# A second layer by Strassen's seven products, with the row normalisation moved ahead of the first layer

## The chip, the cores and the metric

The kernel runs on one core of one Trainium2 chip. The metric is the device time of one execution in microseconds, the lower the better. Before the change three runs took 326.28, 327.08 and 329.61 us, a median of 327.08 us.

## The reference, cut to what matters

Two stages, one after the other: sliding-window attention with a linear bias, then a layer normalisation and two matrix products with a ReLU between them, added to the attention's output.

```python
# q, k, v: (8 batches, 8 heads, 576 rows, 64); window = 128
scores = q @ k.T / 8 + bias          # bias falls with distance, one slope per head
scores = where((rel >= 0) & (rel < window), scores, -1e9)
x = softmax(scores) @ v              # heads side by side: (8, 576, 512)
...
mu, var = mean(x), mean((x - mu) ** 2)
xn = (x - mu) / sqrt(var + 1e-06) * g_ln
ch = maximum(xn @ w_ch1, 0) @ w_ch2  # w_ch1: 512 x 2048, w_ch2: 2048 x 512
out = x + ch
```

## The kernel before

**Blocks.** The 4608 rows are 36 blocks of 128 rows, numbered n = 0 to 35 in the list `order`: nine for each of four pairs of batches. The ninth block of a pair (8, 17, 26, 35; `T` in the code) holds the last 64 rows of both batches.

**Attention of a block.** `turn` transposes the queries and keys of two blocks on TensorE (64 small transposes), into two PSUM banks that DVE and ACT copy out, two copies each. `scores` makes the products of queries and keys (32 matmuls into the banks `ps_sc`), with an exponential on ACT for each half. `masks` multiplies the exponentials by the decay of the bias on DVE, one instruction for each half. `values` multiplies by v on TensorE in two halves of four heads, each into a PSUM bank of its own. On DVE a reciprocal and a scaling then write the half of the fp16 tile x, and the scaling also sums it up (`accum_out`). `centre` makes the mean of these sums, subtracts it (xc), and starts a DMA transpose of xc into the tile xT of the block's group.

**MLP of a group.** Blocks are taken in groups: `GROUPS` has four of 2 blocks, four of 3 and four of 4. `mlp1(g)` makes the 16 slices of the hidden layer: four matmuls each, as wide as the group has rows, then a ReLU on ACT (on DVE for those named in `on_dve`) into `ht`. Since the mean alone is taken off ahead of it, `mlp2(g)` makes 16 matmuls of 512 columns for each block, and `finish` multiplies by the row's `rstd` and adds x in one DVE instruction and issues the two stores on SP's queue. The `rstd` comes from `variance` (two DVE instructions for each block) and `inv_std` (nine small DVE instructions for a whole group: a shift, a subtraction and two Newton steps).

**What sets the order.** The order on TensorE, ACT and DVE is the program's own (`manual_schedule`). Attention is a list of steps, and `weave_at(units, *places)` runs a generator of the MLP unit by unit and puts the next step of that list after each unit named in places. POOL, which issues all loads, and SP, which issues stores and DMA transposes, are put in order by the framework.

**PSUM.** There are eight banks: four belong to the two `ps_sc` tiles, and the four of `ps_mm` are shared by `mlp1`, `mlp2`, `values` and `turn`. A bank is free again when its last reader has ended.

Of the kernel before, what the change touches and what calls it, by code (L numbers as in the profile page):

```python
# [10 lines left out]
FP16 = mybir.dt.float16  # L11
# [11 lines left out]
T = 8  # L23
NSLOT = 9
HALF = P // 2
GROUPS = [2] * 4 + [3] * 4 + [4] * 4

NV = 10
AHEAD = 6
# [28 lines left out]
def kernel(  # L58
# [21 lines left out]
    def pool(name, bufs, **kw):  # L80
        return ctx.enter_context(tc.tile_pool(name=name, bufs=bufs, **kw))
# [2 lines left out]
    raw_pool = pool("raw", 4)  # L84
    turned_pool = pool("turned", 3)
    probs_pool = pool("probs", 4)
    x_pool = pool("x", 14)
    xc_pool = pool("xc", 4)
    small = pool("small", 4)
    group_pool = pool("group", 3)  # L90
    hidden_pool = pool("hidden", 2)
    out_pool = pool("outp", 4)
    ps_scores = pool("ps_scores", 1, space=PSUM)
    ps_mm = pool("ps_mm", 4, space=PSUM)

# [16 lines left out]
    def decay(m, at):  # L112
# [17 lines left out]
    ones = consts.tile([P, 4 * P], FP16)  # L130
    moments = consts.tile([P, NPAIR * NSLOT, nc.vector.BN_AGGR_DIM], FP32)
    rstd = consts.tile([P, NPAIR * NSLOT], FP32)
    w1 = consts.tile([P, NKB, FFN], FP16)
    w1g = consts.tile([P, NKB, FFN], FP16)
    w2 = consts.tile([P, NFB, DM], FP16)
    vext = [
        consts.tile([P, H, D + 1], FP16, name=f"vx{i}", tag=f"vx{i}")
        for i in range(NV)
# [10 lines left out]
    def gain_w1(first, n):  # L149

        for part in range(first, first + n):
            c, kb = divmod(part, NKB)
            cols = slice(c * W1C, (c + 1) * W1C)
            nc.vector.tensor_scalar(
                out=w1g[:, kb, cols],
                in0=w1[:, kb, cols],
                scalar1=g_sb[:, kb : kb + 1],
                scalar2=None,
                op0=ALU.mult,
            )  # L160

    def load_w2(c):
        n = NFB // 4
# [54 lines left out]
            issued += 1  # L218


    xs = {}

    turned = {}

# [101 lines left out]
    def attend(p, blk, keys, mask, tag, hps):  # L326

        heads = slice(2 * hps[0], 2 * hps[-1] + 2)
        nk = len(keys)
        if hps[0] == 0:
            pr = probs_pool.tile([P, H, nk, P], FP16, tag=tag, name=tag)
            for t, o in enumerate(keys):
                weights_of.setdefault((p, blk), []).append((pr, t, o))
        else:
            pr = weights_of[p, blk][-1][0]
        banks = ps_sc[len(scored) % 2]  # L340
        scored.append((p, blk))
        ps = banks.rearrange("p j (n t q) -> p j n t q", n=len(hps), t=nk)
        qt, b = turned["q", p, blk // 2], blk % 2
        for n, hp in enumerate(hps):
            for t, o in enumerate(keys):
                kt = turned["k", p, o // 2][:, o % 2]
                for c, r, queries in seen(p, blk, o, t):
                    cols = slice(c * HALF, (c + 1) * HALF)
                    for j in range(2):
                        rows = slice(j * HALF, (j + 1) * HALF)  # L350
                        nc.tensor.matmul(  # L351
                            in_halves(ps[cols, j, n, t, :])[:, r, queries],
                            kt[rows, hp, cols],
                            in_halves(qt[rows, b, hp])[:, r, queries],
                            start=True,
                            stop=True,
                        )
        dst = pr[:, heads].rearrange("p h t q -> p h (t q)")
        nc.scalar.activation(  # L359
            out=dst.rearrange("p (n j) q -> p j n q", j=2),  # L360
            in_=ps.rearrange("p j n t q -> p j n (t q)"),
            func=AF.Exp,
            scale=inv_sqrt_d,
        )
        unmasked.setdefault((p, blk), []).append((dst, mask[:, heads, :]))
# [23 lines left out]
    def values(p, blk, hg):  # L389

        if hg == 0:
            xs[p, blk] = x_pool.tile([P, DM], FP16, tag="x", name="x")
            sums[p, blk] = small.tile([P, 2], FP32, tag="sum", name="sum")
        ps = ps_mm.tile([P, 4, D + 1], FP32, tag="mm", name="ps_pv")
        terms = weights_of[p, blk]
        for i in range(4):
            h = 4 * hg + i
            for n, (pr, t, o) in enumerate(terms):
                nc.tensor.matmul(  # L399
                    ps[:, i, :],  # L400
                    pr[:, h, t, :],
                    vext[(p * NSLOT + o) % NV][:, h, :],
                    start=(n == 0),
                    stop=(n == len(terms) - 1),
                )
        rec = small.tile([P, 4], FP32, tag="rec", name="rec")
        nc.vector.reciprocal(out=rec, in_=ps[:, :, D])  # L407
        nc.vector.scalar_tensor_tensor(  # L408
            out=xs[p, blk][:, hg * 4 * D : (hg + 1) * 4 * D].rearrange(
                "p (h d) -> p h d", h=4  # L410
            ),
            in0=ps[:, :, 0:D],
            scalar=1.0,
            in1=rec.unsqueeze(2).broadcast_to([P, 4, D]),
            op0=ALU.mult,
            op1=ALU.mult,
            accum_out=sums[p, blk][:, hg : hg + 1],
        )

    turned_x = {}  # L420

    centred = {}

    def centre(p, blk):
# [12 lines left out]
        if p == 0 and blk < FIRST:  # L437
            nc.vector.scalar_tensor_tensor(
                out=xc,
                in0=xs[p, blk],  # L440
                scalar=mean,
                in1=g_row,
                op0=ALU.subtract,
                op1=ALU.mult,
            )
        else:
            nc.vector.tensor_scalar(  # L447
                out=xc, in0=xs[p, blk], scalar1=mean, scalar2=None, op0=ALU.subtract
            )
        n = p * NSLOT + blk  # L450
        g, at = home[n]
        if at == 0:
            turned_x[g] = group_pool.tile([P, NKB, 4 * P], FP16, tag="xT", name="xT")
        if n < BY_DMA:
            centred[p, blk] = xc
        else:
            nc.sync.dma_start_transpose(
                out=turned_x[g][:, :, at * P : (at + 1) * P], in_=xc
            )

    def turn_x(g, at, p, blk, copy):

# [130 lines left out]
    def mlp1(g, on_dve=()):  # L593
# [4 lines left out]
        for fb in range(NFB):  # L598
            ps = ps_mm.tile([P, 4 * P], FP32, tag="mm", name="ps_m1")
            for kb in range(NKB):  # L600
                nc.tensor.matmul(  # L601
# [3 lines left out]
                    start=(kb == 0),  # L605
                    stop=(kb == NKB - 1),
                )
            if fb in on_dve:
# [7 lines left out]
            else:  # L616
                nc.scalar.activation(  # L617
                    out=ht[:, fb, 0:cols], in_=ps[:, 0:cols], func=AF.Relu
                )
            yield cols  # L620

    def mlp2(g, parts=((0, NFB),)):

# [2 lines left out]
        for first, end in parts:  # L626
            for at, (p, blk) in enumerate(members[g]):
# [12 lines left out]
                if end == NFB:  # L640
                    finish(p, blk, sums[at])
                    yield DM

    def finish(p, blk, ps):
        n = p * NSLOT + blk
        o = out_pool.tile([P, DM], FP32, tag="o", name="o")
        nc.vector.scalar_tensor_tensor(  # L647
            out=o,
            in0=ps,
# [2 lines left out]
            op0=ALU.mult,  # L652
            op1=ALU.add,
        )
        for b, t0, w, p0 in spans(p, blk):
            dst, src = out[b, t0 : t0 + w, :], o[p0 : p0 + w, :]
            if blk == T:
# [6 lines left out]
    def weave_at(units, *places, group=None):  # L664


        size = len(members[group]) if group else 0
        first = sum(GROUPS[:group])
        for u, _ in enumerate(units):
            if u % 2 and u // 2 < size:  # L670
                variance(first + u // 2)
                if u // 2 == size - 1:
                    inv_std(first, size)
            advance_to(done + places.count(u))


    nc.vector.memset(ones, 1.0)
# [1 line left out]
        nc.vector.memset(vx[:, :, D : D + 1], 1.0)  # L679
    nc.vector.memset(magic, 0x5F3759DF)  # L680
    nc.vector.memset(one_line, 1.0)
    decay(m_full, 0)
    decay(m_tail, 4)
    load_until(place[3])
    engine = mybir.EngineType
    with tc.manual_schedule(engines={engine.PE}):
        with tc.manual_schedule(engines={engine.Activation, engine.DVE}):
# [6 lines left out]
            weave_at(mlp2(2), 0, 2, 4, 6, 7)  # L694


            weave_at(mlp1(3, (9, 10, 11)), 8, 12)
            weave_at(mlp2(3), 1, 2, 5, 6)
# [35 lines left out]
```

## Time and profile before

| what | value |
|---|---|
| runs, median (three) | 327.08 us (326.28 to 329.61) |
| span of the profiled execution | 326.4 us |
| group 9 (blocks 26 to 29) with its share of attention, 230.69 to 263.94 us | 33.25 us |
| last `mlp1`, 294.10 to 307.91 us | 13.81 us |
| last `mlp2`, 307.91 to 321.74 us | 13.83 us |
| relu of 128x512 on ACT (L617) | 597 ns |
| relu of 128x256 on ACT (L617) | 384 ns |
| copies of a turned block (L267, L268) | DVE 416 and 722 ns, ACT 591 and 761 ns |
| copy of a turned `T` block (L273) | DVE 726 ns, ACT 742 ns |
| small instructions of `inv_std` on DVE | 162 to 170 ns |
| store: issue to landing | 3.0 us |
| DMA transpose of xc: issue to landing | 4.5 us |

The profile shows one execution. PE is TensorE, PEld its weight loads, DVE the vector engine, ACT the scalar engine, POOL the engine that issues the loads, SP the queue for the stores. A line such as L631 is a line of the kernel. "Busy" adds up the durations of instructions; those of matmuls overlap, so the pace of a run of matmuls is read from its length in the chain of waits divided by its number. PEclk is the share of the full clock that TensorE was granted.

### The profile page before, as it was taken

The page shows a single profiled execution, that of the slowest core. Times are in us where ns is not written, and L with a number is a line of the kernel's source. Part 1 is how long each engine was busy: PE and PEld are TensorE (multiplying, and loading weights), DVE is VectorE, ACT ScalarE, POOL GpSimd, SP SyncE. Part 2 cuts the span into 40 slices and gives each one's busy share as a digit, 9 for nine tenths or more (in the row PEclk, how much of TensorE's full clock was granted, in tenths as well). Part 3 has the DMA queues.
Part 4 walks back from the last instruction along what each step waited for, and adds up shares of the span by engine and source line. Part 5 has one row for each costly group of instructions (what it writes and reads, how often), then busy time and mean ns, then how long its engine had stood idle before and what let it go on. Part 6 is the DMA issues. An engine that isn't in the chain of part 4 may idle for free.

```text
span 326.4 us, 9878 instructions
## 1 busy us (share of the span) xinstructions
PE 315.1 (97%) x4190; PEld 181.1 (55%) x4190; DVE 202.4 (62%) x633; ACT 186.3 (57%) x316; POOL 93.1 (29%) x132
## 2 busy tenths in 40 slices
PE   8889999999999999999999999999999999999994
PEld 2468655757655555556565564555455545544441
DVE  2588778776782793688577379459645864436011
ACT  6587756667757557458647547735475537205500
POOL 8823757767120540452332152120000000000000
PEclk9799999999999999999999999999999999999999
DMA  9999999999891996899299299384211430141032
GB/s 113 173 207 192 191 121 167 204 145 134 92 148 30 77 168 83 51 147 134 29 168 129 14 125 157 32 62 90 64 19 18 97 67 18 28 99 36 0 66 64
DMA packets 101726, 32.31 MB, mean 99 GB/s; under 512 B 92849, under 2 KB 97073, under 8 KB 101682
## 3 DMA queue, kind: packets, MB, share of 16 engines
q0 software_dynamic: 79872, 18.36, 68.3%
q1 hardware_dynamic: 21810, 13.32, 21.0%
q8 instruction: 33, 0.54, 0.8%
q14 instruction: 11, 0.09, 0.1%
HBM read 36.90 MB, written 9.44 MB: 142 GB/s over the span
## 4 chain that ended last, share of the span: by engine, by line
PE 85%; DVE 5%; DMA 4%; POOL 3%; issue 1%; POOLq 0%
PE ps_m L631 39%; PE ps_m L601 35%; DMA w<-in_moe_w_ch_dram 4%; PE ps_pv L399 4%; PE ps_sc L351 3%; PE ps_tr L248 3%; DVE x L408 2%; DVE rec L407 1%; POOL q L184 1%; POOL vx L194 1%; POOL k L184 1%; POOL w L145 1%; DVE o L647 0%; PE ps_tx L467 0%; PE ps_sc L248 0%
## 5 line engine op out<-in xcount | busy, mean ns | idle before, releaser
L631 PE MATMUL ps_m<-w,ht 128*128 128x512 f16 x576 | 132.5, 380 | 0.0
L617 ACT ACTIVATE ht<-ps_m 128x384 f16<-128x384 f32 (+2 forms) x183 | 89.8, 491 | 55.3 <-PE ps_m L601 52.7
L601 PE MATMUL ps_m<-xT,w1g 128*128 128x512 f16 (+2 forms) x640 | 114.3, 337 | 0.2 <-DVE probs L370 0.2
L601 PEld LDWEIGHTS <-w1g 128*128 128x128 f16 x640 | 61.8, 98 | 49.1 <-issue 0.8
L631 PEld LDWEIGHTS <-ht 128*128 128x128 f16 x576 | 53.4, 98 | 59.8
L359 ACT ACTIVATE probs<-ps_sc 128x1024 f16<-128x1024 f32 x56 | 54.2, 1021 | 46.2 <-PE ps_sc L351 46.1
L194 POOL DMA_DIRECT2D vx<-in_v_dram x40 | 33.9, 855 | 86.4 <-PE ps_pv L399 54.4
L407 DVE RECIPROCAL rec<-ps_pv 128x4 f32<-128x4 f32 x72 | 12.9, 180 | 63.5 <-PE ps_pv L399 63.3
L647 DVE SCALAR_TENSOR_TENSOR o<-ps_m,rstd,x 128x512 f32<-128x512 f32 x36 | 26.7, 745 | 29.9 <-PE ps_m L631 29.9
L370 DVE TENSOR_TENSOR probs<-probs,m 128x1024 f16<-128x1024 f16 x56 | 36.4, 682 | 1.6 <-ACT probs L359 1.3
L184 POOL DMA_DIRECT2D q<-in_q_dram x40 | 27.1, 684 | 28.2 <-PE ps_tr L248 21.3
L408 DVE SCALAR_TENSOR_TENSOR x<-ps_pv,rec 128x256 f16<-128x256 f32 x72 | 30.5, 424 | 2.5
L184 POOL DMA_DIRECT2D k<-in_k_dram x40 | 26.9, 685 | 5.1 <-DMA w<-in_moe_w_ch_dram 3.1
L472 DVE BATCH_NORM_STATS2 st<-x 128x6 f32<-128x512 f16 x36 | 24.1, 668 | 0.0
L399 PEld LDWEIGHTS <-probs 128*128 128x128 f16 x448 | 18.7, 97 | 6.6 <-DVE probs L370 0.3
L351 PE MATMUL ps_sc<-q,k 64*64 64x128 f16 (+1 forms) x1088 | 20.1, 210 | 0.7 <-ACT probs L359 0.4
L399 PE MATMUL ps_pv<-vx,probs 128*128 128x65 f16 x448 | 20.1, 193 | 0.0
L359 ACT ACTIVATE own<-ps_sc 128x1024 f16<-128x1024 f32 x12 | 11.9, 1030 | 11.8 <-PE ps_sc L351 11.8
L351 PEld LDWEIGHTS <-k 64*64 64x64 f16 x1088 | 14.8, 109 | 5.9 <-issue 3.5
L601 PE MATMUL ps_m<-xT,w 128*128 128x256 f16 x128 | 15.1, 273 | 0.4 <-ACT ht L617 0.2
L601 PEld LDWEIGHTS <-w 128*128 128x128 f16 x128 | 12.0, 98 | 2.1 <-DMA w<-in_moe_w_ch_dram 0.8
L447 DVE TENSOR_SCALAR xc<-x,mean 128x512 f16<-128x512 f16 x32 | 12.0, 375 | 1.1
(57 smaller groups left out, 190.3 us busy)
## 6 DMA issues: line engine op xcount, KB each, us to landing
out_dram<-o SPq DMA_DIRECT2D x72, 128.0 KB, 3.0
q<-in_q_dram POOLq DMA_DIRECT2D x32, 128.0 KB, 5.4
k<-in_k_dram POOLq DMA_DIRECT2D x32, 128.0 KB, 5.8
vx<-in_v_dram POOLq DMA_DIRECT2D x32, 128.0 KB, 5.9
w<-in_moe_w_ch_dram POOLq DMA_DIRECT2D x8, 512.0 KB, 12.4
q<-in_q_dram POOLq DMA_DIRECT2D x8, 64.0 KB, 5.4
k<-in_k_dram POOLq DMA_DIRECT2D x8, 64.0 KB, 4.7
vx<-in_v_dram POOLq DMA_DIRECT2D x8, 64.0 KB, 4.5
```

The lines of the kernel that those rows point to most:

```text
L184: nc.gpsimd.dma_start(out=t[b * n // 2 : (b + 1) * n // 2], in_=src[2 * p + b, :, i * P : i * P + n, :].rearrange("h (c r) d -> c h r d", ...
L194: nc.gpsimd.dma_start(out=vx[p0 : p0 + n, :, 0:D], in_=v[b, :, t0 : t0 + n, :].rearrange("h p d -> p h d"),)
L351: nc.tensor.matmul(in_halves(ps[cols, j, n, t, :])[:, r, queries], kt[rows, hp, cols], in_halves(qt[rows, b, hp])[:, r, queries], start=Tr ...
L359: nc.scalar.activation(out=dst.rearrange("p (n j) q -> p j n q", j=2), in_=ps.rearrange("p j n t q -> p j n (t q)"), func=AF.Exp, scale=in ...
L370: nc.vector.tensor_tensor(out=dst, in0=dst, in1=mask, op=ALU.mult)
L399: nc.tensor.matmul(ps[:, i, :], pr[:, h, t, :], vext[(p * NSLOT + o) % NV][:, h, :], start=(n == 0), stop=(n == len(terms) - 1),)
L408: nc.vector.scalar_tensor_tensor(out=xs[p, blk][:, hg * 4 * D : (hg + 1) * 4 * D].rearrange("p (h d) -> p h d", h=4), in0=ps[:, :, 0:D], s ...
L472: nc.vector.bn_stats(out=st, in_=xs[order[n]])
L601: nc.tensor.matmul(ps[:, 0:cols], w[:, kb, fb * P : (fb + 1) * P], xT[:, kb, 0:cols], start=(kb == 0), stop=(kb == NKB - 1),)
L617: nc.scalar.activation(out=ht[:, fb, 0:cols], in_=ps[:, 0:cols], func=AF.Relu)
L631: nc.tensor.matmul(sums[at], ht[:, fb, at * P : (at + 1) * P], w2[:, fb, :], start=(fb == 0), stop=(fb == NFB - 1),)
L647: nc.vector.scalar_tensor_tensor(out=o, in0=ps, scalar=rstd[:, n : n + 1], in1=xs[p, blk], op0=ALU.mult, op1=ALU.add,)
```

## The change

The 28 blocks from block 8 on are computed in another way; the first eight stay as they were.

- Groups become six of 2 blocks and six of 4. Groups 4 to 11 (`FAST` = 4) use the new second layer.
- `stats(n)` and `normal(n)` take the place of `centre` and `inv_std` for these blocks: mean and variance by `variance` on DVE, two small POOL instructions (an addition and a power) for `rstd`, and one DVE instruction that subtracts and scales, followed by the DMA transpose. Each block's attention is now three steps (V: values, scores, turn; M: masks and stats; N: normal) where it was two. The sum of `accum_out` and the mean fall away.
- `combine_w2` makes four combinations of the quarters of w2, once, on DVE: eight instructions of 128x1024, woven into `mlp1(4)`. Three go into memory of w1, one over a quarter of w2 itself.
- `combine_hidden` makes four sums of quarters of `ht` for each group, in two halves: eight DVE instructions, four after unit 10 of `mlp1`, four in `fast_mlp2`. For these groups `mlp1` makes the slices of the two halves of the hidden layer in turns.
- `fast_mlp2` makes seven products of half-size matrices in place of eight. Each has 8 matmuls of 256 columns for each pair of rows' blocks. Three of the products add to the bank of an earlier one (`x`, `z`), after DVE has read it. Eight additions on DVE take the banks over into the output tiles; the four blocks' stores go out in two lots.
- The places in `weave_at` are new, and no ReLU of groups 4 to 11 runs on DVE.

```diff
-GROUPS = [2] * 4 + [3] * 4 + [4] * 4
+GROUPS = [2] * 6 + [4] * 6
+FAST = 4
...
+            for dst, a, b in (
+                (t1, quarter(0, 1), quarter(0, 0)),
+                (t2, quarter(1, 1), t1),
+                (t3, quarter(1, 1), quarter(0, 1)),
+                (t4, quarter(1, 0), t2),
+            ):
+                nc.vector.tensor_tensor(
+                    out=dst[:, f], in0=a[:, f], in1=b[:, f], op=ALU.subtract
+                )
+                yield
...
+    def normal(n):
+        xc = xc_pool.tile([P, DM], FP16, tag="xc", name="xc")
+        nc.vector.tensor_scalar(
+            out=xc,
+            in0=xs[order[n]],
+            scalar1=moments[:, n, 0:1],
+            scalar2=rstd[:, n : n + 1],
+            op0=ALU.subtract,
+            op1=ALU.mult,
+        )
+        nc.sync.dma_start_transpose(out=group_tile(n), in_=xc)
+
+    def stats(n):
+        variance(n)
+        here = rstd[:, n : n + 1]
+        nc.gpsimd.tensor_tensor(
+            out=here, in0=moments[:, n, 1:2], in1=powers[:, 0:1], op=ALU.add
+        )
+        nc.gpsimd.tensor_tensor(out=here, in0=here, in1=powers[:, 1:2], op=ALU.pow)
...
-        step = first_half + second_half
+        step = first_half + second_half[:1]
...
-        steps.append([m for t in (n + 1, n + 2) if t < count for m in masks_of(t)])
+        steps.append(
+            [m for t in (n + 1, n + 2) if t < count for m in masks_of(t)] + [(stats, n)]
+        )
+        steps.append([(normal, n)])
...
+            if g >= FAST and u == 10:
+                for i in range(4):
+                    combine_hidden(g, 0, i)
...
+        dst, a, b, op = (
+            (s1, a21, a22, ALU.add),
+            (s2, s1, a11, ALU.subtract),
+            (s4, a12, s2, ALU.subtract),
+            (s3, a11, a21, ALU.subtract),
+        )[i]
+        nc.vector.tensor_tensor(out=dst[:, f], in0=a[:, f], in1=b[:, f], op=op)
...
+        def product(name, lhs, rhs, first):
+            if first:
+                banks[name] = ps_mm.tile([P, 2, QD], FP32, tag="mm", name="ps_f")
+            for pair in range(pairs):
+                for fb in range(QF):
+                    nc.tensor.matmul(
+                        banks[name][:, pair, :],
+                        lhs[:, fb, pair * P : (pair + 1) * P],
+                        rhs[:, fb, :],
...
+                yield DM
...
+        combine_hidden(g, 1, 0)
+        combine_hidden(g, 1, 1)
+        yield from product("x", a[0][0], quarter(0, 0), True)
+        add("x", 0, 0, True)
+        combine_hidden(g, 1, 2)
+        yield from product("y", a[0][1], quarter(1, 0), True)
+        add("y", 0, 0, False)
+        combine_hidden(g, 1, 3)
+        yield from product("z", s[0], t1, True)
+        add("z", 1, 1, True)
+        yield from product("x", s[1], t2, False)
+        add("x", 0, 1, True)
+        yield from product("z", s[3], quarter(1, 1), False)
+        add("z", 0, 1, False)
+        send(0)
+        yield from product("x", s[2], t3, False)
+        add("x", 1, 0, True)
+        add("x", 1, 1, False)
+        yield from product("w", a[1][1], t4, True)
+        add("w", 1, 0, False)
+        send(1)
...
-            for g in range(4, len(GROUPS)):
-                in_first = g in (6, 8, 9, 10)
-                weave_at(mlp1(g, (9,) * in_first), *(8, 10) * in_first, group=g)
-                weave_at(mlp2(g), *((1, 2, 5, 6, 9, 10) if g < 10 else (1, 2, 5, 6)))
+            weave_at(mlp1(3, (9, 10, 11)), 8, 12, 13)
+            weave_at(mlp2(3), 0, 1, 2, 4, 5, 6)
+            for g in range(4, 6):
+                weave_at(mlp1(g), 1, 4, 6, 8, 11, 13, also=range(0, 16, 2) if g == 4 else ())
+                weave_at(fast_mlp2(g), 1, 3, 5)
+            for g in range(6, len(GROUPS)):
+                weave_at(mlp1(g), 1, 2, 5, 7, 9, 12, 14)
+                weave_at(fast_mlp2(g), 3, 6, 8, 9, 13)
```

More of the change, by code (lines that the diff above doesn't have):

```diff
@@ L135 @@
     w2 = consts.tile([P, NFB, DM], FP16)
+    QF, QD = NFB // 2, DM // 2
+    hsum = [consts.tile([P, QF, 2 * P], FP16, name=f"hs{i}", tag=f"hs{i}") for i in range(2)]
+    spare = [w1[:, i, :].rearrange("p (f d) -> p f d", d=QD) for i in range(4)]
+    hsum.append(spare[3])
     vext = [
@@ L160, in gain_w1, with quarter, combine_w2 @@
             )
+    def quarter(i, j):
+        return w2[:, i * QF : (i + 1) * QF, j * QD : (j + 1) * QD]
+    t1, t2, t4 = spare[:3]
+    t3 = quarter(0, 1)
+    def combine_w2():
+        for part in range(2):
+            f = slice(part * QF // 2, (part + 1) * QF // 2)
+            for dst, a, b in (
[8 more added lines that the diff above has]
+                yield
     def load_w2(c):
@@ L416, in values @@
             op1=ALU.mult,
-            accum_out=sums[p, blk][:, hg : hg + 1],
+            **(
+                dict(accum_out=sums[p, blk][:, hg : hg + 1])
+                if (p, blk) in sums
+                else {}
+            ),
         )
@@ L597, in mlp1 @@
         ht = hidden[g] = hidden_pool.tile([P, NFB, 4 * P], FP16, tag="ht", name="ht")
-        for fb in range(NFB):
+        turn_about = chain(*zip(range(QF), range(QF, NFB)))
+        for u, fb in enumerate(turn_about if g >= FAST else range(NFB)):
             ps = ps_mm.tile([P, 4 * P], FP32, tag="mm", name="ps_m1")
@@ new lines, in fast_mlp2, with rows, add, send @@
+    def fast_mlp2(g):
+        pairs = len(members[g]) // 2
+        n0 = sum(GROUPS[:g])
+        outs = [out_pool.tile([P, 2, DM], FP32, tag="o", name="o") for _ in range(2)]
+        def rows(i):
+            if pairs == 1:
+                return x_pairs[n0 // 2][:, i : i + 1, :], outs[0][:, i : i + 1, :]
+            return x_pairs[n0 // 2 + i], outs[i]
+        banks = {}
+        def product(name, lhs, rhs, first):
[7 more added lines that the diff above has]
+                        rhs[:, fb, :],
+                        start=(first and pair == 0 and fb == 0),
+                        stop=(fb == QF - 1),
+                        skip_group_check=True,
+                    )
+                yield DM
+        def add(name, i, j, to_x):
+            x, o = rows(i)
+            cols = slice(j * QD, (j + 1) * QD)
+            nc.vector.tensor_tensor(
+                out=o[:, :, cols],
+                in0=banks[name][:, 0:pairs, :],
+                in1=(x if to_x else o)[:, :, cols],
+                op=ALU.add,
+            )
+        def send(i):
+            _, o = rows(i)
+            for at in range(pairs):
+                store(*members[g][i * pairs + at], o[:, at, :])
+        a = [[hidden_quarter(g, i, j) for j in range(2)] for i in range(2)]
+        s = [hidden_sum(g, i) for i in range(4)]
+        combine_hidden(g, 1, 0)
[19 more added lines that the diff above has]
+        send(1)
@@ L662, in finish, with weave_at @@
                     nc.sync.dma_start(out=dst[r], in_=src[r * HALF : (r + 1) * HALF])
-    def weave_at(units, *places, group=None):
-        size = len(members[group]) if group else 0
-        first = sum(GROUPS[:group])
+    def weave_at(units, *places, also=()):
         for u, _ in enumerate(units):
[L670 to L673, printed above, removed]
             advance_to(done + places.count(u))
+            if u in also:
+                next(combined, None)
     nc.vector.memset(ones, 1.0)
```

60 lines of the change are left out of this document (39 added, 21 removed).

## The prediction

> **What bounds the kernel now.** First the page's busy times and slices, then the chain that ended last, by line.
>
> ```profile
> PE 315.1 (97%) x4190; PEld 181.1 (55%) x4190; DVE 202.4 (62%) x633; ACT 186.3 (57%) x316; POOL 93.1 (29%) x132
> PE   8889999999999999999999999999999999999994
> PEclk9799999999999999999999999999999999999999
> PE ps_m L631 39%; PE ps_m L601 35%; DMA w<-in_moe_w_ch_dram 4%; PE ps_pv L399 4%; PE ps_sc L351 3%; PE ps_tr L248 3%; DVE x L408 2%; DVE rec L407 1%; POOL q L184 1%; POOL vx L194 1%; POOL k L184 1%; POOL w L145 1%; DVE o L647 0%; PE ps_tx L467 0%; PE ps_sc L248 0%
> ```
>
> TensorE is busy throughout at full clock; the second layer (L631) is 39% of the chain. Matmul durations overlap, so the pace comes from the chain in order of time (start, length, what).
>
> ```profile
> 28.23 7.87 PE ps_m L601 x72
> ...
> 307.91 13.83 PE ps_m L631 x64
> ...
> 321.76 0.75 DVE o L647
> ```
>
> A matmul of 512 columns costs 13.83/64 = 216.1 ns and one of 256 columns 7.87/72 = 109.3 ns, each with its own weight load. Next the stages: length, busy time of PE, PEld, DVE, ACT and POOL, granted clock, DMA, GB/s. The last two rows are from the start of the run.
>
> ```profile
> 94.64:120.11 25.47, 25.38 (x353) 15.12 (x354) 16.16 (x52) 15.34 (x25) 7.08 (x10) 1.00 0.86 91
> 230.69:263.94 33.25, 33.16 (x418) 17.52 (x416) 21.15 (x65) 18.46 (x26) 0.00 (x0) 1.00 0.25 50
> ...
> 8.00:10.00 2.00, 1.40 (x34) 0.79 (x33) 0.66 (x2) 0.71 (x1) 2.00 (x3) 0.64 1.95 161
> 10.00:12.00 2.00, 2.00 (x36) 0.97 (x35) 0.63 (x2) 0.71 (x2) 1.83 (x4) 0.51 1.93 170
> ```
>
> In a four-block group (second row) TensorE has 33.16 of 33.25 us and DVE 21.15, or 64%. That third of DVE is all the room that the change has. The prices on DVE:
>
> ```profile
> L370 DVE TENSOR_TENSOR probs<-probs,m 128x1024 f16<-128x1024 f16 x56 | 36.4, 682 | 1.6 <-ACT probs L359 1.3
> L408 DVE SCALAR_TENSOR_TENSOR x<-ps_pv,rec 128x256 f16<-128x256 f32 x72 | 30.5, 424 | 2.5
> L647 DVE SCALAR_TENSOR_TENSOR o<-ps_m,rstd,x 128x512 f32<-128x512 f32 x36 | 26.7, 745 | 29.9 <-PE ps_m L631 29.9
> L472 DVE BATCH_NORM_STATS2 st<-x 128x6 f32<-128x512 f16 x36 | 24.1, 668 | 0.0
> L407 DVE RECIPROCAL rec<-ps_pv 128x4 f32<-128x4 f32 x72 | 12.9, 180 | 63.5 <-PE ps_pv L399 63.3
> L447 DVE TENSOR_SCALAR xc<-x,mean 128x512 f16<-128x512 f16 x32 | 12.0, 375 | 1.1
> L473 DVE BATCH_NORM_AGGREGATE moments<-st 128x2 f32<-128x6 f32 x36 | 6.6, 182 | 1.3
> ```
>
> Last the timeline of one turned block and of the end.
>
> ```profile
> 248.14 1.94 ACT L359 ACTIVATE probs<-ps_sc 128x1024 f16<-128x1024 f32 x2 [1.93 <-PE ps_sc L351]
> 249.96 0.59 ACT L267 COPY q<-ps_tr 128x512 f16<-128x512 f16 x1
> 250.29 1.28 DVE L370 TENSOR_TENSOR probs<-probs,m 128x1024 f16<-128x1024 f16 x2
> 250.43 0.77 ACT L268 COPY k<-ps_tr 128x512 f16<-128x512 f16 x1
> ...
> 322.54 1.11 SPq L658 DMA_DIRECT2D out_dram<-o  x2
> ```
>
> **What TensorE saves.** Before, 28 blocks x 16 matmuls x 216.1 ns = 96.8 us. After, 28 matmuls of 256 columns for each block: 784 x 109.3 ns = 85.7 us. Gain 11.1 us. Other widths keep their price per column (10.40 us for 64 of 384 columns, 162.5 ns).
>
> [...]
>
> **What DVE gains and loses.** A new sum of 1024 fp16 elements has the form of L370: 682 ns. One of 512 I take at 415, being 682 less half of the 512 columns' worth (0.52 ns each). An addition out of PSUM of 512 fp32 lies between L647's 745 and the 674 ns of the copy into g_row: 690; of 256 columns, 420. For a four-block group this gives 8 reciprocals 1.4, 8 scalings 3.4, two turned blocks' copies 2.3, 8 masks 5.5, statistics 3.4, normal 1.5, and new 8 sums 5.5 and 8 additions 5.5. That is 28.4 us of DVE against TensorE's 64 x 216.1 + 112 x 109.3 ns + 5.3 of attention = 31.4. Room remains, but 90% of an engine that takes its work in order will be late in places.
>
> Groups 4 and 5 are worse. Each has two blocks of MLP but three of attention (V12 to V14, V15 to V17). Group 4: reciprocals 1.1, scalings 2.5, copies 1.9, masks 4.1, statistics 2.6, normal 1.1, sums 3.3, additions 3.4, and the eight combinations of w2 5.5: 25.4 us. Group 5: 19.7 us. TensorE needs (64 + 56) x 109.3 ns + 4.2 = 17.3 us for each. DVE's excess is 45.1 - 34.7 = 10.4 us, and it reaches TensorE: z of group 4 needs the first sum, which stands behind all of that, and `values` need their banks back. I add 1.3 us for DVE's own waits (for POOL, for products): **loss 11.7**. Lower bound: a pair of masks took 1.28 instead of 1.36, so 6% off the total, and 2 us of it may slip into group 6: 5.7. Upper bound 16.
>
> **Banks in groups 7, 8 and 9.** Here V with a turn follows y. TensorE would do values 0.48, scores 0.47 and turn 0.69, and start z 1.64 us after y. But x and y hold two of the four banks (y's addition stands behind V's work on DVE), values and then turn have the other two, and in the order of the built kernel z's first matmul waits for ACT: it gets the bank that ACT copies out last. That is 0.48 + 0.24 for half of the scores + 0.18 + 1.94 exponentials + 0.59 + 0.77 copies + 0.1 = 4.3 us after y: 2.7 lost in groups 7 and 8, and 2.0 in 9, whose `T` block has one copy of 742 ns. **Loss 7.4.** Before, the same V stood inside one open sum, which needs no new bank, and hid this.
>
> **In order on DVE, group 6.** Ahead of V20's reciprocal stand M19, N19, four sums and an addition; z waits 0.8 us for its bank, and the turn behind V21 another 1.0. **Loss 1.8.** N waits for POOL's two small instructions. No row has these: DVE's of 128x4 take 162 ns, POOL's load issues 684 to 855. I take 0.8 us for the pair, between 0.3 and 1.7; one such wait in a group is uncovered, so the ends are 3 us less and 5 us more in all. POOL's queued loads wait meanwhile, but they run six blocks ahead.
>
> **The rest.** In `mlp2(3)` N9 stands behind POOL and ahead of V10's reciprocal, whose banks the turn needs: 1.1. ACT takes over the last ReLUs: 16 x 0.60 + 2 x 1.94 + 1.4 = 14.9 us beside 16.2 of TensorE in `mlp1` of group 8, hidden. At the end four stores are issued in place of two, 0.55 us each: 1.1; the last addition (0.69) replaces `finish` (0.75). Powers' memsets (about 0.1) lie before the first load lands. What DVE no longer does (mean 214 ns, accumulator read 83, Newton steps 165) is already left out of the counts above.
>
> **Sum.** -11.1 + 11.7 + 7.4 + 1.8 + 1.1 + 1.1 = +12.0 on a span of 326.4: 338.4. The median of the runs lies 0.7 above the span: 339.
>
> **Rivals.**
> 1. *Faster (0.22).* DVE's additions and sums end ahead of the products everywhere, so TensorE is never held: 326.4 - 11.1 + 1.1 + 0.7 = 317, up to 323 with part of the bank waits. For it: DVE sits idle 38% now, and neighbours start before the last one ends. It decides at all losses together under 7.8 us; the bank waits alone are 7.4, and groups 4 and 5 would need instructions a quarter shorter than their rows.
> 2. *No change (0.13).* DVE keeps to the lower bound in groups 4 and 5 and the other ends are low: losses 10 to 12, 324 to 329.
> 3. *Much slower (0.05).* The two rows with clock 0.64 and 0.51 show that TensorE loses half its clock for 4 us after a sparse stretch; that costs 2 us. One in each of groups 4 to 9 adds 12: 351. For it: z of group 4 waits 3.5 us by my walk. Against: the other waits are at most 2.7.
>
> [...] The trace shows the drop in the two rows, but not which gap sets it.
>
> **How the numbers follow.** The forecast has 0.60, with a range of its own from 331 to 346 by the ends above. Over all cases 320 to 346 leaves out about half of rival 1, rival 3 and the tail: 0.18. About 1% is what a measurement here can tell from no change; below 323.8 lies 0.22, up to 330.3 another 0.13, and above it 0.65.
>
> **What would show it.** DVE near 240 us in all, 42 or more of 47 us busy in groups 4 and 5, which would take 47 in place of 35; TensorE idle for DVE ahead of group 4's z (3 us and more) and for ACT's copies ahead of z in groups 7, 8 and 9; the last `fast_mlp2` 12.2 us against 13.83. I am wrong if 256-column matmuls differ from 109 ns, if z doesn't wait there, or if DVE has idle time in group 4.

## The result and the profile after

The changed kernel takes 336.44 us (median of four runs, 336.04 to 337.82), the kernel before 326.89 beside it. The ratio is 1.029, with a 95% interval from 1.0245 to 1.0335: slower. The profiled execution has a span of 334.7 us against 326.4, or 8.3 more.

The page of the changed kernel, the lines that answer to those shown of before: busy times, slices of TensorE and its clock, and the chain that ended last by line.

```profile
PE 307.1 (92%) x4526; PEld 214.8 (64%) x4526; DVE 241.9 (72%) x583; ACT 184.8 (55%) x320; POOL 115.8 (35%) x188
...
PE   8889999999897698899999979997999999999992
...
PEclk9999999999999899999999999999999999999998
...
PE ps_m L664 30%; PE ps_f L756 22%; PE ps_m L697 7%; ACT probs L389 4%; PE ps_pv L433 4%; PE ps_sc L381 3%; DVE probs L400 3%; DVE x L442 2%; PE ps_tr L277 2%; DMA k<-in_k_dram 2%; DVE st L530 2%; DVE hs L732 1%; DVE w L186 1%; ACT k L297 1%; DVE o L769 1%
```

TensorE is busy 8.0 us less, and idle 334.7 - 307.1 = 27.6 us where it was idle 11.3: 16.3 us more. DVE is on the chain now. The slices show where: 13, 14 and 16 lie in groups 4 and 5, one of them with a lower clock (8 in the row PEclk), and single slices follow later on. The stages in figures, with the columns length, then busy time of PE, PEld, DVE, ACT and POOL, granted clock, DMA share, GB/s. The rows are `mlp2(3)`, group 4, group 5 and group 7.

```profile
84.36:95.40 11.04, 9.53 (x186) 5.44 (x184) 9.04 (x22) 6.35 (x10) 5.23 (x9) 1.00 0.64 76
95.40:120.69 25.29, 20.15 (x362) 16.75 (x360) 22.73 (x54) 13.39 (x26) 11.14 (x17) 0.93 0.98 82
120.69:141.91 21.22, 18.61 (x386) 15.67 (x384) 18.03 (x49) 12.69 (x25) 11.63 (x20) 1.00 1.17 108
174.76:208.53 33.77, 31.65 (x466) 22.21 (x464) 25.61 (x56) 18.42 (x27) 11.79 (x20) 1.00 0.85 99
```

In groups 4 and 5, 7.75 us of 46.51 have no TensorE work at all. Group 7 had 2.1 idle, group 8 the same. The end, from the chain in order of time:

```profile
316.62 12.24 PE ps_f L756 x112
...
328.88 0.69 DVE o L769
```

12.24 us for 112 matmuls is 109.3 ns each, and 1.59 us less than the 13.83 of the plain layer: the product side is as priced. Behind the last addition come 334.7 - 329.57 = 5.1 us, where before had 326.4 - 322.51 = 3.9.

Now the waits, in the timeline of one value product in `mlp2(3)`:

```profile
86.30 0.18 DVE L531 BATCH_NORM_AGGREGATE moments<-st 128x2 f32<-128x6 f32 x1
...
86.56 0.19 POOL L485 TENSOR_TENSOR rstd<-moments,powers 128x1 f32<-128x1 f32 x1 [5.76 <-DVE moments L531]
...
86.83 0.55 POOL L488 TENSOR_TENSOR rstd<-rstd,powers 128x1 f32<-128x1 f32 x1
...
87.42 0.41 DVE L472 TENSOR_SCALAR xc<-x,moments,rstd 128x512 f16<-128x512 f16 x1 [0.94 <-POOL rstd L488]
87.74 0.17 DVE L441 RECIPROCAL rec<-ps_pv 128x4 f32<-128x4 f32 x1
...
88.52 0.44 PE L277 MATMUL ps_tr<-iden,q 64*64 64x64 f16 x30 [1.51 <-DVE rec L441]
```

The statistics end at 86.48, GpSimd makes rstd in two instructions, and the normalisation (L472) can't start before 87.42. DVE takes its work in order, so it stands idle for 0.94 us with the next block's reciprocal and scaling, both ready, behind the waiting instruction. The bank that they would free is the one TensorE's transposes need: TensorE waits 1.51 us. In the run with the normalisation one value product later (below) this wait is 0.19 us, and `mlp2(3)` takes 9.72 us in place of 11.04. The two other large waits, by the timeline of TensorE:

```profile
113.28 0.61 PE L756 MATMUL ps_f<-w,hs 128*128 128x256 f16 x4 [2.48 <-DVE hs L732]
...
198.74 1.47 PE L756 MATMUL ps_f<-w,hs 128*128 128x256 f16 x12 [1.55 <-ACT k L297]
```

The first is z of group 4, waiting for a hidden sum; the second is z of group 7, waiting for the bank that ACT copies out last.

### The profile page after: what moved, and what is told of

Same layout as the page of the kernel before. It is cut to its first block, busy times and chain, and to the rows that moved or that the text cites. A ratio compares the mean times of both kernels' runs of the same rounds, so it can differ in the third digit from the quotient of the medians.

```text
span 334.7 us, 10542 instructions
## 1 busy us (share of the span) xinstructions
PE 307.1 (92%) x4526; PEld 214.8 (64%) x4526; DVE 241.9 (72%) x583; ACT 184.8 (55%) x320; POOL 115.8 (35%) x188
## 4 chain that ended last, share of the span: by engine, by line
PE 69%; DVE 16%; ACT 6%; POOL 3%; issue 2%; DMA 2%; POOLq 0%; DVEq 0%
PE ps_m L664 30%; PE ps_f L756 22%; PE ps_m L697 7%; ACT probs L389 4%; PE ps_pv L433 4%; PE ps_sc L381 3%; DVE probs L400 3%; DVE x L442 2%; PE ps_tr L277 2%; DMA k<-in_k_dram 2%; DVE st L530 2%; DVE hs L732 1%; DVE w L186 1%; ACT k L297 1%; DVE o L769 1%
## 5 line engine op out<-in xcount | busy, mean ns | idle before, releaser
L664 PE MATMUL ps_m<-xT,w1g 128*128 128x512 f16 (+1 forms) x640 | 117.4, 337 | 5.0 <-ACT k L297 3.4
L680 ACT ACTIVATE ht<-ps_m 128x512 f16<-128x512 f32 (+1 forms) x187 | 90.4, 498 | 56.8 <-PE ps_m L664 50.6
L756 PE MATMUL ps_f<-w,ht 128*128 128x256 f16 x448 | 51.5, 273 | 0.5 <-DVE o L769 0.5
L756 PEld LDWEIGHTS <-ht 128*128 128x128 f16 x448 | 43.5, 98 | 7.5 <-issue 0.9
L756 PE MATMUL ps_f<-w,hs 128*128 128x256 f16 x224 | 26.7, 276 | 5.9 <-ACT k L297 3.0
L697 PE MATMUL ps_m<-w,ht 128*128 128x512 f16 x128 | 31.0, 380 | 0.0
L756 PEld LDWEIGHTS <-hs 128*128 128x128 f16 x224 | 21.9, 99 | 9.2 <-issue 3.1
L769 DVE TENSOR_TENSOR o<-ps_f,x 128x512 f32<-128x512 f32 (+1 forms) x32 | 19.7, 615 | 10.3 <-PE ps_f L756 10.3
L472 DVE TENSOR_SCALAR xc<-x,moments,rstd 128x512 f16<-128x512 f16 x28 | 11.5, 412 | 18.2 <-POOL rstd L488 18.2
L769 DVE TENSOR_TENSOR o<-ps_f,o 128x512 f32<-128x512 f32 (+1 forms) x32 | 19.4, 612 | 3.8 <-PE ps_f L756 3.7
```

Source lines behind the costliest of these rows:

```text
L664: nc.tensor.matmul(ps[:, 0:cols], w[:, kb, fb * P : (fb + 1) * P], xT[:, kb, 0:cols], start=(kb == 0), stop=(kb == NKB - 1),)
L680: nc.scalar.activation(out=ht[:, fb, 0:cols], in_=ps[:, 0:cols], func=AF.Relu)
L697: nc.tensor.matmul(sums[at], ht[:, fb, at * P : (at + 1) * P], w2[:, fb, :], start=(fb == 0), stop=(fb == NFB - 1),)
L756: nc.tensor.matmul(banks[name][:, pair, :], lhs[:, fb, pair * P : (pair + 1) * P], rhs[:, fb, :], start=(first and pair == 0 and fb == 0), ...
L769: nc.vector.tensor_tensor(out=o[:, :, cols], in0=banks[name][:, 0:pairs, :], in1=(x if to_x else o)[:, :, cols], op=ALU.add,)
```

## The experiments

Each short diff is against the changed kernel, unless another is named. All times are medians, and the kernel before lay between 326.68 and 327.08 us beside them.

**The value product one unit later** (groups 6 to 11):

```diff
-                weave_at(fast_mlp2(g), 3, 6, 8, 9, 13)
+                weave_at(fast_mlp2(g), 4, 6, 8, 9, 13)
```

> In groups 6 to 11 the step V of the second layer stands one unit later, between the two halves of product z, so that z takes its bank before values and turn take theirs. Theory of the banks: z no longer waits for ACT's last copy (3.89 us from y's end to z in group 7, 3.72 in group 8, against 1.5 of TensorE's own work); 2.3 us come back in groups 7 and 8 and about 1 in group 9, where the wait was partly for DVE: 330.5 to 332 us, and TensorE's waits for ACT's copies ahead of products go from 3.0 us to 0. Rival, DVE's order: the sums and additions behind V are late anyway, so the wait only moves to the next product: 335 to 337 us.

334.0 us, ratio 1.0225 (1.0189 to 1.0261): 2.4 us less, between the two expectations. Groups 7, 8 and 9 took 32.50, 32.45 and 32.85 us in place of 33.77, 33.57 and 32.94, which is 2.5 us, and no z waits for ACT any more. So the mechanism is right and its price about half of what was expected.

**Without the sums of w2.** This leaves out the eight subtractions of w2's quarters, so the products read other weights.

```diff
-    combined = combine_w2()
+    combined = iter(())
```

> The eight combinations of w2 are left out (the products use what lies in their places). Theory of DVE's amount: group 4 takes 25.3 us with DVE busy for 22.7; without 5.4 us of it the wait of 2.5 us ahead of z goes, and with it the clock's drop behind it (25.3 us at a mean of 0.93, so 1.8 us): group 4 near 20 us, total 330.5 to 331.5. Rival, waiting and not work: DVE's queue is held by single waits, so that less work leaves the same waits: group 4 near 24 us, total 334.5 to 335.5.

332.71 us, ratio 1.0196 (1.0139 to 1.0253), between the two expectations. Group 4 fell from 25.29 to 20.43 us, 4.9 us for 5.4 us of DVE work: z no longer waits, and the clock stays at 1.00 where its mean was 0.93. Group 5 stayed at 21.15. In the profiled execution the clock fell to 0.50 in group 7 instead, which took 35.44 us in place of 33.77, so the time shows less than group 4 gave back.

**The rstd of the block before.** The normalisation reads the previous block's rstd, so it waits for nothing new; the values are another block's.

```diff
-            scalar2=rstd[:, n : n + 1],
+            scalar2=rstd[:, n - 1 : n],
```

> Each block is scaled by the rstd of the block before it, so that DVE no longer waits for POOL's two instructions of the same block, which still run. Theory of DVE's amount: of the 18.2 us that DVE waits for POOL only 1.7 lie in groups 4 and 5 and 11.0 in groups 6 to 9, where TensorE waits mostly for ACT's copies: 333 to 335 us. Rival, the wait for POOL is the cause: these 13 us stand in DVE's order ahead of the sums and the reciprocals that TensorE waits for, and half or more of them come back: 330 us or less.

334.77 us, ratio 1.0244 (1.0206 to 1.0282). The 1.51 us wait fell to 0.68, and group 3 took 18.22 us in place of 19.68. GpSimd's pair is not the main loss in this kernel.

**Without the hidden sums.** The sums of the hidden layer's quarters are left out; the products read single quarters.

```diff
-        nc.vector.tensor_tensor(out=dst[:, f], in0=a[:, f], in1=b[:, f], op=op)
```

> The sums of the hidden layer's quarters are left out; the products read the quarters themselves, and all matmuls, additions and w2 combinations stay. DVE loses 39 us. Theory of DVE's amount: groups 4 and 5 lose 3.4 us of DVE each, group 4 loses its wait ahead of z and the clock's drop; in groups 6 to 9 the wait for the bank of z stays, since ACT ends it, and only the waits for DVE ahead of turns go: 327 to 330 us. Rival, nothing but the sums stands in the way: all of the saved 11.1 us of TensorE shows: 319 us or less.

332.76 us, ratio 1.0182 (1.0146 to 1.0218), a miss: 64 instructions and, by the page's busy times, 34.6 us of DVE work are gone and 3.7 us come back. Only group 4 became shorter, by 3.3 us. Group 5 took 21.14 us and group 6 32.84, as with the sums (21.22 and 32.85). Whatever holds TensorE there isn't the amount of DVE work; the longest wait in group 5 is 1.47 us for ACT's copy of the keys, with the sums and without. Taking out single parts of the scheme had given back 3.7 us at most, so the next kernels took the scheme out altogether, or left the order as it was and moved the scheme.

**The order alone.** Group sizes, steps and normalisation of the changed kernel, with the plain second layer in all groups; `finish` only adds for blocks 8 to 35.

```diff
-FAST = 4
+FAST = 12
...
-                weave_at(mlp1(g), 1, 4, 6, 8, 11, 13, also=range(0, 16, 2) if g == 4 else ())
-                weave_at(fast_mlp2(g), 1, 3, 5)
+                weave_at(mlp1(g), 1, 4, 6, 8, 11, 13)
+                weave_at(mlp2(g), 1, 3, 5)
...
-                weave_at(fast_mlp2(g), 3, 6, 8, 9, 13)
+                weave_at(mlp2(g), 4, 7, 8, 9, 13)
```

> The changed kernel with its group sizes and its normalisation ahead of the first layer, but with the plain second layer everywhere (eight quarter products, no sums of w2 or of the hidden layer; what the addition at the end multiplies by before is already in the hidden layer, so it only adds). TensorE has the 11.1 us of the eighth products again. Theory: the loss is two things, the scheme's sums in group 4 and the new order; with the sums gone the order still costs the 1.1 us in the second layer of group 3, waits for ACT's copies in groups 4 and 5 (1.5 us or so each) and about 1 us in each group of four: 331 to 334 us. Rival: the order is free and everything lost belongs to the scheme: 327 to 328.5 us, as before the change. A second rival, that the order is the main loss and the scheme is a net gain of some 5 us or more: 337 us or above, slower than the changed kernel.

337.98 us, ratio 1.0304 (1.0256 to 1.0352): the second rival. The order without the scheme costs as much as the whole change. Its timeline in the second layer of group 6 shows the same round trip, made longer by a load that GpSimd issues first:

```profile
164.68 0.88 POOL L223 DMA_DIRECT2D vx<-in_v_dram  x1 [4.45 <-PE ps_pv L433]
...
166.45 0.41 DVE L472 TENSOR_SCALAR xc<-x,moments,rstd 128x512 f16<-128x512 f16 x1 [1.51 <-POOL rstd L488]
...
167.56 0.44 PE L277 MATMUL ps_tr<-iden,q 64*64 64x64 f16 x30 [2.66 <-DVE rec L441]
```

Behind that wait the clock fell to 0.50 and 0.65 in the two stretches of 2 us that followed, and group 6 took 37.73 us where 64 + 64 matmuls at 216.1 ns and 5.3 us of attention make 33.0.

**The scheme from group 6 on.** Groups 4 and 5 take the plain layer, with other places for their attention steps; the sums of w2 are spread over the first layers of groups 4 to 6, and the value product of the large groups stands as in the first experiment.

```diff
-FAST = 4
+FAST = 6
...
-                weave_at(fast_mlp2(g), 1, 3, 5)
+                weave_at(mlp2(g), 1, 2, 4, 5, 6)
...
-                weave_at(fast_mlp2(g), 3, 6, 8, 9, 13)
+                weave_at(fast_mlp2(g), 4, 6, 8, 9, 13)
```

> Groups 4 and 5 (two blocks each) take the plain second layer, which costs TensorE 2 x 0.8 us; the six groups of four keep the scheme. The sums of w2 are spread over the first layers of groups 4, 5 and 6, and the value product in the second layer of the groups of four stands after the first product of z, as in v_after_y. Theory (the scheme is paid for in the two small groups, where the sums meet too little TensorE time): groups 4 and 5 take 39 to 41 us in place of 46.5, groups 7 and 8 some 32.5 in place of 33.7, and the time is 325 to 328.5 us, within 1 per cent of before. Rival (the new order is what costs, with or without the sums): groups 4 and 5 stay over 43 us and the time is 330 us or more.

329.01 us, ratio 1.0058 (1.0031 to 1.0085), half a microsecond above the theory's range and below the rival's. Groups 4 and 5 took 20.85 and 20.75 us, 41.60 together in place of 46.51, though TensorE has 1.6 us more to do there.

**The sums of w2 on GpSimd**, with the value product as in the first experiment.

```diff
-                nc.vector.tensor_tensor(
+                nc.gpsimd.tensor_tensor(
```

> The eight subtractions of w2 issued on GpSimd in place of VectorE, and the value product after the first product of z as in v_after_y. Theory (the amount of VectorE work in group 4): the 3.7 us of no_w2_sums and the 2.4 us of v_after_y add up, 330 to 331.5 us, with group 4 at 20.5 to 21.5 us. Rival: on GpSimd the subtractions take so long that the first product that reads them waits, or they slow VectorE's own work beside them: group 4 stays over 23.5 us and the time is 333 us or more.

343.44 us, ratio 1.0459 (1.0407 to 1.0511). The rival's numbers were met (333 us or more; group 4 took 24.21), but neither expectation had it right about where most of the time went. GpSimd's instructions are put in order by the framework, which took six of the eight subtractions forward to the stretch from 55 to 72 us. The timeline there, in which the long row is a centring of 128x512:

```profile
61.38 2.14 POOL L186 TENSOR_TENSOR w<-w,w 128x1024 f16<-128x1024 f16 x1
...
62.25 7.62 DVE L513 TENSOR_SCALAR xc<-x,mean 128x512 f16<-128x512 f16 x1
...
65.54 6.38 POOL L186 TENSOR_TENSOR w<-w,w 128x1024 f16<-128x1024 f16 x3
```

The centring took 7.62 us beside them, where the four in the changed kernel take 0.38 to 0.75. The first layer of group 3 started at 84.88 us, not near 76.

**The order alone, normalisation one value product later** (against the order alone):

```diff
-        step = first_half + second_half[:1]
+        step = first_half + second_half[:1] + [(normal, n - 1)] * (n > 8)
...
-        steps.append([(normal, n)])
+        steps.append([(normal, n)] * (n == count - 1))
```

> order_alone with one edit: a block's normalisation stands behind the value product of the next block on VectorE, not ahead of it, so that the round trip from VectorE to GpSimd and back (sums of squares, the pair for rstd, then the normalisation) is no longer in front of the reciprocal that TensorE's next transposes wait for. In order_alone TensorE waited 1.5 us in group 3 and 2.7 us ahead of group 6 for it, with a dropped clock behind the second. Theory (this round trip is the largest part of what the order costs): both waits go, group 3 is back to 18.2 us, group 6 to some 33.3 us, and the time falls by 5 to 6.5 us, to 331.5 to 333. Rival (the length of the steps in group 6 has another reason, the banks or the transposes' landing): the time stays over 335.5 us.

332.25 us, ratio 1.017 (1.014 to 1.02): 5.7 us less, as the theory had it. Group 3 took 17.74 us, group 6 34.17. So half of what the order costs is the round trip standing in front of work that was ready, with the clock of 0.50 behind it.

**The scheme from group 6, with the same edit:**

> scheme_from_6 with the same edit. There TensorE waited 4.5 us in seven places for the reciprocal. Theory: the waits fall under 1.5 us and the time by 2 to 3 us, to 326 to 327 us, no more than 0.2 per cent from before. Rival (what is moved behind the value product comes too late for the next first layer, or holds VectorE's copy of the turned queries): no gain, 328.5 us or more.

324.65 us, ratio 0.9924 (0.9907 to 0.9941): faster than before, and 4.4 us less than without the edit, more than the theory's 2 to 3. TensorE's waits for the reciprocal fell from 4.5 to 1.1 us. The four stages from group 4 to group 7:

```profile
93.46:113.31 19.85, 18.45 (x337) 13.48 (x338) 15.35 (x36) 13.26 (x25) 10.13 (x16) 1.00 1.22 102
113.31:133.59 20.28, 18.71 (x362) 13.41 (x360) 15.41 (x36) 13.26 (x26) 11.05 (x18) 1.00 1.20 111
133.59:166.09 32.50, 31.55 (x481) 21.90 (x480) 26.30 (x58) 18.98 (x28) 14.06 (x23) 1.00 1.02 87
166.09:198.32 32.23, 31.61 (x466) 22.14 (x464) 25.97 (x56) 18.42 (x27) 12.34 (x20) 1.00 0.94 104
```

The last two rows have as much DVE work as group 7 of the changed kernel (25.61 us) and little idle TensorE: 26 us of DVE in 32 is no harm if it is in an order that nobody waits for.

**The turn out of the small first layers** (against the kernel of the last experiment, groups 4 and 5):

```diff
-                weave_at(mlp1(g), 1, 4, 6, 8, also=(10, 12, 14))
-                weave_at(mlp2(g), 1, 2, 4, 5, 6)
+                weave_at(mlp1(g), 1, 15, also=(10, 12, 14))
+                weave_at(mlp2(g), 0, 1, 2, 4, 5, 5, 6)
```

> from_6_normal_later with one more edit: in groups 4 and 5 the value product with its turn stands after the last product of the first layer, no longer after the fifth, so that the next bank is wanted by the plain second layer, which stays in one bank for 16 products. Theory (in the small groups the first layer takes a new bank every 0.44 us and so meets ACT's copy of the keys, 1.3 us in each): both waits go, 2.5 us less than from_6_normal_later, 324 to 325 us, faster than before. Rival (three value products in the second layer are more than VectorE can follow there, 5 us each in 7 us): the waits go to VectorE's results and the time does not fall.

324.26 us, ratio 0.9912 (0.9878 to 0.9946). The first layers of groups 4 and 5 no longer wait for ACT's copies, and the two groups took 38.51 us in place of 40.13. In place of those waits stand shorter ones for DVE's results (0.49, 0.55 and 0.60 us), which the rival had named. The time fell by 0.4 us, inside both intervals: the expected 2.5 us did not come.

**The changed kernel, normalisation one value product later**, the two lines as above:

> The changed kernel with one edit: a block's normalisation behind the value product of the next block on VectorE, as in order_normal_later. Theory (the round trip to GpSimd costs the changed kernel what its own trace shows: the 1.5 us wait in group 3, some 1 us of shorter ones, and with less clock lost a little more): 2 to 3.5 us less than the changed kernel, 333 to 334.5 us; the rest of the gap to from_6_normal_later, 6 to 8 us, is the sums in the small groups and the place of the value product. Rival (in the changed kernel VectorE is so full that the later place gives nothing): 335.5 us or more.

333.88 us (four runs, 332.57 to 338.9), ratio 1.0186 (1.0146 to 1.0226), 2.6 us less, as the theory had it. In the trace group 3 is 1.95 us shorter; group 4 is 1.65 shorter, with the clock at 1.00, and group 7 is 1.67 longer, since the clock falls to 0.50 there instead. Group 4 still took 23.64 us and group 5 21.15.

**Two queues for the last stores** (against the turn outside; two of the last four stores go to ScalarE's queue):

```diff
-                for r in range(2):
-                    nc.sync.dma_start(out=dst[r], in_=src[r * HALF : (r + 1) * HALF])
+                for r, queue in enumerate((nc.sync, other)):
+                    queue.dma_start(out=dst[r], in_=src[r * HALF : (r + 1) * HALF])
```

> from_6_turn_outside with one edit: of the four stores behind the last addition two are issued by ScalarE in place of all four by SyncE. Theory (the end is as long as the stores that are issued one after another): 0.6 to 1.2 us less behind the last addition, 323 to 323.7 us, some 1 per cent faster than before. Rival (the end is the landing of the last store, however it is issued): no difference, 324 to 324.6 us.

323.29 us, ratio 0.9883 (0.986 to 0.9906). In the traces 4.7 us lie behind the last addition in place of 5.2. The interval overlaps that of the kernel without the edit, so no more than these 0.5 us is shown. This is the best version, 1.2% faster than the kernel before.

## Why the prediction came out, and where its steps failed

**TensorE's saving, 11.1 us: right.** 216.1 and 109.3 ns held, and the last second layer was 1.59 us shorter, seven times over for the 28 blocks.

**`mlp2(3)`, 1.1: about right.** It was 1.3 longer than with the later normalisation (11.04 against 9.72), by the mechanism named.

**Groups 4 and 5, 11.7: the sum was right, its cause only in part.** 46.51 us against the 34.7 of TensorE's own work is 11.8. The step was "DVE's excess is 45.1 - 34.7 = 10.4 us, and it reaches TensorE". DVE was busy 40.8 us, because neighbours overlap, and had 2.6 us idle in group 4, which the prediction named as a sign against itself. Three kernels with the same places in `weave_at` divide the 11.8 like this. 4.9 go with the sums of w2 (46.51 to 41.58), all in group 4; 1.7 of them are the lowered clock behind z's wait. Another 2.4 go when the plain layer takes the place of the scheme (41.58 to 40.73, and 1.6 of TensorE's saving that is given up with it). 4.5 are left in the order alone (40.73 against 36.2), and 2.8 of these are products of the first layer that wait for ACT's copies of the keys; there a new bank is wanted every 0.44 us. The later normalisation gave these two groups nothing in that order (40.74), and 1.5 in the kernel with the scheme from group 6 (41.60 to 40.13). Group 5 isn't held by DVE's amount: without 2.4 us of that work (18.03 to 15.66 us busy) it was as long as with it.

**Banks in groups 7, 8 and 9, 7.4: mechanism right, size wrong.** The three lost 6.1 us against 31.4 each, but only 2.5 of it went with the later value product. z waited for ACT's copies in groups 7 and 8 (1.55 and 1.4 us); in group 9 it did not. Most of the other 3.6 us were still there in every version with the later value product (32.2 to 32.9 us a group), so they are not this wait. In the kernel with the scheme from group 6 and the later normalisation they are 2.9, of which the profile lists 2.1 as six waits of 0.2 to 0.5 us: transposes for DVE's reciprocal or scaling, and in group 9 a product for ACT's copy.

**Group 6, 1.8, and the end, 1.1: about right.** 32.85 us against 31.4 is 1.5; behind the last addition there were 1.2 us more.

**The sum, +12.0 on the span: too high by 3.7.** The lengths by stage were met: the prediction's 47 us for groups 4 and 5 was 46.5. But losses were counted from an undisturbed TensorE and added to a span that has losses too: groups 4 to 9 of the kernel before took 169.3 us, where the same prices make 166.9. Those 2.4 us were never deducted. Losses of 21.9 in place of 23.1 make up most of the rest.

**Rival 1, faster,** failed by the waits, and **rival 2, no change,** needed losses of 10 to 12. **Rival 3, a lost clock in each of groups 4 to 9,** came true once, in group 4, the one whose z was expected to wait longest: the slice with 8 in the row PEclk, 3.41 us at 0.50, or 1.7 us. The two rows that it rested on don't show a sparse stretch: in the 3.42 us ahead of that drop, which is 3.41 us at 0.50 from 8.55 on, TensorE was busy for 2.93.

**What no step had.** The prediction laid most of the loss at the scheme's DVE work. About half belongs to the new order: with the plain layer it costs 11.3 us over the kernel before (337.98 against 326.68). On top of that the scheme in all 28 blocks gains 1.5 us of its 11.1, which is within the intervals, so it loses the other half itself. With the order mended, and only in the six large groups, it gains 7.6 (332.25 to 324.65) of 24 x 0.395 = 9.5; in the traces each of the six is 0.8 to 1.7 us shorter. The prediction gave the wait for GpSimd a pair of 0.8 us and one uncovered wait in a group at most. The pair is 0.22 + 0.57 us by the page's means, but DVE's wait was 0.94 us in `mlp2(3)` and 1.51 behind a load of 0.88 in the order alone, and its cost depends on what stands behind it on DVE. Not separated: the order alone, mended, still costs 5.3 us over the kernel before, and groups 4 and 5 alone take 4.5 more than their plain products and attention (40.74 us against 36.2). Whether groups of two in place of three or the normalisation's place ahead of the first layer is the reason was not tried.

## What to carry to other kernels

When a step is moved to the front of a chain and handed to another engine, look at what stands behind the waiting instruction on its in-order engine: one edit of two lines, consumer behind the next ready work, was worth 2.6 to 5.7 us here. A scheme that trades matmuls for sums pays in stages where TensorE has time to hide them: here the groups of four gained, the groups of two took 0.9 us more than with the plain layer even without the sums of w2, and these sums, made once, cost 4.9 us in the small group where they were put. Before a loss is laid at the new arithmetic, run the new order with the old arithmetic.

## What was not expected of the hardware

**The clock fell after gaps as short as 1.6 us, and not always.** Two stretches of 3.41 us in group 7 of the changed kernel with the later normalisation, columns as above:

```profile
191.40:194.82 3.42, 1.34 (x69) 1.23 (x70) 2.80 (x8) 2.93 (x4) 2.95 (x5) 1.00 0.47 42
194.82:198.23 3.41, 3.41 (x19) 2.41 (x17) 0.90 (x3) 0.00 (x0) 0.35 (x1) 0.50 1.46 119
```

The gap is 1.58 us and lies in the first row, with 1.34 us of TensorE work beside it. The clock was 0.50 throughout the second and 1.00 after it, and the group took 35.44 us. The same wait in the changed kernel (1.55 us) left the clock at 1.00 and the group at 33.77; without the sums of w2 the clock fell to 0.50 after 1.55 us too. Gaps of 2.48 and 2.66 us were each followed by 3.41 us at 0.50. What tells these cases apart in the traces is not the gap but TensorE's busy time in a stretch of 3.41 us, when the stretches are counted off without a break from the drops of the same trace. Ahead of a drop it was 0.75 us (order alone), 0.88 (changed kernel, group 4), 1.15 (value product later), 1.34 (above), 1.37 (without the sums of w2), 1.43 (sums on GpSimd) and 1.57 (rstd of the block before). In the changed kernel the stretch with the wait of 1.55 us had more:

```profile
196.26:199.67 3.41, 1.62 (x71) 1.54 (x72) 2.32 (x5) 2.43 (x4) 3.08 (x5) 1.00 0.89 67
199.67:203.08 3.41, 3.41 (x33) 3.06 (x32) 2.39 (x4) 0.00 (x0) 0.00 (x0) 1.00 0.61 56
```

So in these traces a wait cost clock or not by how it lay in the stretches so counted. Counted from another start, one in the changed kernel has less TensorE work than there was ahead of four of the seven drops, and the clock stayed at 1.00 in it and behind it:

```profile
195.45:198.86 3.41, 1.29 (x98) 1.09 (x87) 2.46 (x7) 3.05 (x4) 2.54 (x4) 1.00 0.51 36
```

The border isn't sharp: 1.57 us left the clock at 1.00 without the hidden sums, and 1.51 us did at the end of the version with two queues. The drop at the start of the kernel before, with 2.93 us of work ahead of it, doesn't fit at all. TensorE worked in each of these stretches. A wholly idle one came only with the sums of w2 on GpSimd (63.00 to 66.41 us), and the clock fell behind it as well; its mean over that run was 0.979, against 0.992 in the changed kernel. What sets the drop, no run here shows.

**An instruction of DVE took 7.62 us beside GpSimd's work.** A subtraction of 1024 fp16 elements took 2.12 us on GpSimd against 0.67 on DVE. The centring of 128x512 beside them, 0.38 to 0.75 us in the changed kernel, lasted from 62.25 to 69.87 us, through the ends of four of GpSimd's instructions. What made it so long, no run here shows.
